# A fused attention and expert kernel: GpSimd takes the division of the probabilities in batch 0's attention, VectorE half of the copies to xT, and the global block's transposes another PSUM pool

## Chip, cores and metric

One core of a Trainium2 chip runs the whole program. The metric is the device time of one execution in microseconds, the median of three runs. The engines are PE (TensorE, with PEld for its weight loads), DVE (VectorE), ACT (ScalarE), POOL (GpSimd) and SP, whose queue issues the DMAs.

## What is computed

The reference is attention with a local window and a few global keys, followed by a mixture of eight experts whose gate is balanced by eight rounds of row and column scaling, followed by one dense feed-forward layer. Everything is float32. There are 2 batches of 768 positions, 8 heads of width 64, 8 global keys and a window of 96.

```python
def _attn_ref(q, k, v, n_global, n_local):
    scores = scale * np.matmul(q, k.transpose(0, 1, 3, 2))
    ...
    scores = np.where(keep, scores + bias, -1e9)      # keep: global key, or 0 <= i - j < n_local
    a = np.exp(scores - np.max(scores, axis=-1, keepdims=True))
    a = a / (np.sum(a, axis=-1, keepdims=True) + 1e-09)
    return np.matmul(a, v).astype(np.float32)

x = attn_out.transpose(0, 2, 1, 3).reshape(1536, 512)
# _moe_ref
for e in range(8):
    out += P[:, e:e + 1] * (np.maximum(x @ w1[e], 0.0) @ w2[e])     # w1[e] 512x1024
# _moe2_ref
h = out @ w_in                                                      # 512x2048
return (h * (1.0 / (1.0 + np.exp(-1.702 * h))) @ w_out).astype(np.float32)
```

## The kernel before

**Numbers.** Every product is made of three float32r products: an operand is split into a high part `h` and a rest `l`, and `l*h + h*l + h*h` is accumulated in PSUM. `split` (L207) makes the pair: the high part on the engine named by `eng`, the rest, a subtraction, on GpSimd or VectorE.

**Attention in tiles.** A tile is 128 queries of two heads, `(b, hp, i)`: batch, pair of heads (0 to 3), and one of six tiles. `work` lists them in this order, so batch 0 is the first 24. Below, tile 15 is `work[15]`, which is (0, 2, 3) and appears in names as `2_3`. A tile sees its own 128 keys, the 128 before, and 32 that hold the global ones: 288 columns, 256 for i=1 and 128 for i=0. Its steps are these:

- `scores`: six matmuls, then for each of the two heads VectorE adds the bias and finds the row's maximum (L1014) and ScalarE takes the exponential and the row's sum `rs` (L1017).
- `norm`: VectorE adds 1e-9 to `rs` (L1024), takes the reciprocal (L1025) and multiplies the two heads' probabilities by it (two instructions of L1027).
- `turn`: PE transposes the probabilities into the bank `pt` (L1038) and, from i=2 on, the global block into `pg` (L1046). ScalarE copies them out (`ah`, `ag`). The function that it returns makes the rest `al` on VectorE (L1059).
- `values`: PE multiplies by v into `pv` (L1079). After every odd i, `put_x` copies the two heads of two tiles to xT, here called `xf`, by two instructions on ScalarE (L851).

**The loop.** Step n of the loop at L1097 handles four tiles at once: the scores of tile n, the division of tile n-1, the transposes of tile n-3 and the product with v of tile n-4. The string `ORDER[self.phase]` says in which order (`t` turn, `s` scores, `v` values, `r` the rest, `n` norm). The order of instructions on each engine is the order in which the program writes them. After steps with i=1 and i=4 `prep_qk` transposes the next half pair's keys and queries (`pk`, `pq`), after i=2 and i=5 `prep_v` splits v on GpSimd (L214, L216).

**What is woven in.** `scores`, `values` and others are generators, and at their yields the loop in `path` (L1230) moves two others on: `first`, which prepares the first expert weights on GpSimd (sums, splits, and at the end the splits `w2h`/`w2l`), and `early`, which prepares the expert's operands from `xf` (`B11`, `T1`, later `B21`, `B22`, `T2` to `T4`, several of them through L298 and L216 on GpSimd). `self.phase` is 1 while tiles 0 to 21 leave through `values`, thus through batch 0's attention. Then the mixture starts (phase 2 and 3), in which batch 1's attention is woven into the expert products of batch 0, and later only expert and dense products are left.

**Banks.** PSUM has four pools of banks: `ps_s` 2, `ps_t` 2, `ps_v` 1, `ps_m` 3. `psum` (L638) chooses by a letter. In phase 1 the scores take `ps_m`, `pk` and `pq` take `ps_s`, and `pt` and `pg` take turns in `ps_t`.

Of the kernel before, what the change touches and what calls it, by code (L numbers as in the profile page):

```python
# [11 lines left out]
AF = mybir.ActivationFunctionType  # L12
ALU = mybir.AluOpType
# [3 lines left out]
P = 128  # L17
GK = 32
# [6 lines left out]
LR = 2  # L25


ORDER = {1: "tsvrn", 2: "stnrv", 3: "stnrv"}


def f(t):
    return t.bitcast(F32)
# [16 lines left out]
class Kernel:  # L49
# [588 lines left out]
    def psum(self, kind, shape, name):  # L638

        if kind == "r":  # L640
            kind = "m" if self.idle else "t"
        if kind == "2":
            self.turnover += 1
            kinds = {2: "m", 3: "sst", 4: "sstt"}[self.phase]
            kind = kinds[self.turnover % len(kinds)]
        elif self.phase == 1:
            kind = {"s": "m", "p": "s"}.get(kind, kind)
        kind = "t" if kind == "p" else kind
        p = {"s": self.ps_s, "t": self.ps_t, "v": self.ps_v, "m": self.ps_m}[kind]
        return p.tile(shape, F32, tag=kind, name=name)  # L650

# [190 lines left out]
    def put_x(self, pv, b, hp, i):  # L842


        nc = self.nc
        if hp == 0 and i == 1:
            self.xf = self.xfp.tile([P, self.DC, self.S], F32, tag="xf", name=f"xf_{b}")
        ts_ = slice((i - 1) * P, (i + 1) * P)
        for j in range(2):
            r = slice(64 * j, 64 * j + 64)  # L850
            nc.scalar.activation(self.xf[r, hp, ts_].rearrange("p (s t) -> p s t", s=2), pv[r, :, j, :], AF.Copy)  # L851

    def slope(self, h):
        return 2.0 ** -(8.0 * (h + 1) / self.H)
# [166 lines left out]
    def norm(self, b, hp, i):  # L1021
        nc = self.nc
        a, rs, wn = self.aa[b, hp, i]
        nc.vector.tensor_scalar(rs, rs, 1e-9, None, op0=ALU.add)  # L1024
        nc.vector.reciprocal(rs, rs)  # L1025
        for j in range(2):
            nc.vector.tensor_scalar(a[:, j, :wn], a[:, j, :wn], rs[:, j : j + 1], None, op0=ALU.mult)  # L1027

    def turn(self, b, hp, i):

        nc = self.nc
        a, _, _ = self.aa.pop((b, hp, i))
        n = 1 if i == 0 else 2
        pt = self.psum("t", [P, n, 2, P], f"pt_{b}_{hp}_{i}")
        for j in range(2):
            for c in range(n):
                o = c * (P if i == 1 else SLOT)
                nc.tensor.transpose(pt[:, c, j, :], a[:, j, o : o + P], self.ident)  # L1038
        ah = self.a_t.tile([P, 2, 2, P], F32R, tag="ah", name=f"ah_{b}_{hp}_{i}")
        al = self.a_t.tile([P, 2, 2, P], F32R, tag="al", name=f"al_{b}_{hp}_{i}")  # L1040
        nc.scalar.activation(ah[:, :n], pt, AF.Copy)
        ag = None
        if i >= 2:
            pg = self.psum("t", [GK, 2, P], f"pg_{b}_{hp}_{i}")
            for j in range(2):
                nc.tensor.transpose(pg[:, j, :], a[:, j, P:SLOT], self.ident)  # L1046

            if b == 0:
                ag = self.a_t.tile([GK, 2, P], F32, tag="ag", name=f"ag_{b}_{hp}_{i}")
                nc.scalar.activation(ag, pg, AF.Copy)  # L1050
            else:

                ag = self.a_t.tile([3 * GK, 2, P], F32R, tag="ag", name=f"ag_{b}_{hp}_{i}")
                nc.scalar.activation(ag[:GK], pg, AF.Copy)
                nc.scalar.activation(ag[2 * GK :], pg, AF.Copy)
        self.at[b, hp, i] = ah, al, ag

        def rest():
            nc.vector.tensor_tensor(out=al[:, :n], in0=pt, in1=f(ah)[:, :n], op=ALU.subtract)  # L1059
            if ag is not None and b > 0:  # L1060
                nc.vector.tensor_tensor(out=ag[GK : 2 * GK], in0=pg, in1=f(ag)[:GK], op=ALU.subtract)

        return rest
# [19 lines left out]
    def attention_banded(self):  # L1083

        nc = self.nc
        self.aq, self.av, self.vg = {}, {}, {}
        self.aa, self.at = {}, {}
        pairs = [(b, hp) for b in range(self.B) for hp in range(self.HP)]
        work = [(b, hp, i) for b, hp in pairs for i in range(self.NT)]
        tables = self.tables()  # L1090
        next(tables)
        self.scales()
        self.counts()
        next(tables)
        yield from self.prep_qk(0)
        next(tables)
        for n in range(len(work) + LV):  # L1097
            b, hp, i = work[n] if n < len(work) else (None, None, None)
            pair = n // self.NT
            rest = None  # L1100
            for o in ORDER[self.phase]:
                if o == "s" and i is not None:
                    yield from self.scores(b, hp, i)
                    if n == 0:
                        self.prep_v(0)
                if o == "t" and LT <= n < len(work) + LT:
                    rest = self.turn(*work[n - LT])
                if o == "n" and 1 <= n <= len(work):
                    self.norm(*work[n - 1])
                if o == "r" and rest is not None:  # L1110
                    rest()
                    yield
                if o == "v" and n >= LV:
                    self.values(*work[n - LV])
                    yield work[n - LV]
            if i == 1:
                yield from self.prep_qk(2 * pair + 1)
            if i == 4 and pair + 1 < len(pairs):
                yield from self.prep_qk(2 * pair + 2)
            if i == 2:  # L1120
                self.prep_v(2 * pair + 1)
            if i == 5 and pair + 1 < len(pairs):
                self.prep_v(2 * pair + 2)
# [246 lines left out]
```

## Time and profile before

| | |
|---|---|
| median of 3 runs | 1449.24 us (1448.56 to 1450.29) |
| profiled execution, its own time | 1451.42 us |
| its span, first to last instruction | 1449.5 us |
| busy share of the span: PE, DVE, POOL, ACT | 97%, 69%, 59%, 44% |
| mean granted TensorE clock | 0.993 |
| chain that ended last, by engine | PE 83%, DVE 10%, ACT 4%, issue 2%, POOL 1% |

The profiled execution is one more run, and what lies around its span is 1.92 us. Busy shares are means over all stages: batch 0's attention fills only about the first 95 us. The granted clock is 1.0 at 2.4 GHz and 0.5 at 1.2 GHz.

### The profile page before, as it was taken

How to read it: one execution, taken by the hardware profiler on the slowest of the kernel's cores; microseconds unless marked ns; L12 is line 12 of the kernel's file. 1: busy time of each engine (PE TensorE's matmuls, PEld its weight loads, DVE VectorE, ACT ScalarE, POOL GpSimd, SP SyncE). 2: the span in 40 equal slices, each digit the busy share in tenths (PEclk: the TensorE clock that was granted, in tenths of full speed). 3: DMA queues.
4: the chain of work that ended last, by engine and by line, in shares of the span. 5: the costliest groups of instructions: out<-in, count | busy, mean ns of one | idle time of the engine just before them, and what ended most of it. 6: DMA issues, size and time to landing. Idle time of an engine off the chain costs nothing.

```text
span 1449.5 us, 20861 instructions
## 1 busy us (share of the span) xinstructions
PE 1403.4 (97%) x7295; PEld 1239.3 (86%) x7295; DVE 1003.4 (69%) x1880; ACT 638.6 (44%) x1528; POOL 855.0 (59%) x999
## 2 busy tenths in 40 slices
PE   6899999899999999999999999999999988999998
PEld 5568888788898998998998998998989977898997
DVE  7987886667767777777677777777655464556655
ACT  5676766343443343333343333343333365444332
POOL 4755555756875666554666555666554567566642
PEclk9999999999999999999999999999999999999999
DMA  6322210111131222221222221222100100010002
GB/s 154 76 59 62 72 49 31 59 59 59 64 118 58 71 84 88 73 74 51 85 76 87 73 70 55 83 77 87 45 30 29 45 29 16 30 44 30 30 1 88
DMA packets 92626, 89.53 MB, mean 62 GB/s; under 512 B 41824, under 2 KB 70496, under 8 KB 92512
## 3 DMA queue, kind: packets, MB, share of 16 engines
q1 hardware_dynamic: 92512, 88.12, 19.5%
q8 instruction: 59, 0.97, 0.3%
q14 instruction: 55, 0.45, 0.1%
HBM read 76.56 MB, written 11.53 MB: 61 GB/s over the span
## 4 chain that ended last, share of the span: by engine, by line
PE 83%; DVE 10%; ACT 4%; issue 2%; POOL 1%; POOLq 0%; DVEq 0%; ACTq 0%
PE pl L558 41%; PE pl1y L503 11%; PE pl1x L503 11%; PE pl1z L503 10%; PE pl1w L503 5%; PE pv L1079 2%; PE s L1001 1%; DVE hl L482 1%; DVE a L1027 1%; DVE u L455 1%; DVE a L1014 1%; DVE al L1059 1%; PE pt L1038 1%; ACT hh L479 1%; PE plg L373 0%
## 5 line engine op out<-in xcount | busy, mean ns | idle before, releaser
L569 DVE SCALAR_TENSOR_TENSOR acc<-pl,pr,acc 128x512 f32<-128x512 f32 x312 | 233.4, 749 | 117.4 <-PE pl L558 115.2
L558 PE MATMUL pl<-w2h,hl 128*128 128x512 f32 x960 | 301.6, 395 | 5.9 <-DVE accx L567 2.4
L558 PE MATMUL pl<-w2h,hh 128*128 128x512 f32 x960 | 297.6, 391 | 3.3 <-ACT hh L210 2.8
L558 PE MATMUL pl<-w2l,hh 128*128 128x512 f32 x960 | 297.5, 391 | 0.0
L216 POOL TENSOR_TENSOR w2l<-r,w2h 128x512 fp32r<-128x512 f32 x96 | 128.7, 1362 | 194.4 <-ACT w2h L210 181.3
L558 PEld LDWEIGHTS pl<-w2h,hh 128*128 128x128 f32 x960 | 180.3, 188 | 42.7 <-ACT hh L210 3.1
L558 PEld LDWEIGHTS pl<-w2l,hh 128*128 128x128 f32 x960 | 180.5, 188 | 39.4
L558 PEld LDWEIGHTS pl<-w2h,hl 128*128 128x128 f32 x960 | 176.4, 188 | 40.1 <-DVE accx L567 3.8
L210 ACT ACTIVATE w2h<-r 128x512 fp32r<-128x512 f32 x94 | 54.3, 625 | 193.9 <-PE pl L558 163.0
L477 POOL TENSOR_TENSOR hl<-u,hh 128x384 fp32r<-128x384 f32 x100 | 106.9, 1078 | 38.4 <-ACT hh L474 38.2
L510 ACT ACTIVATE p<-pl1x 128x384 f32<-128x384 f32 x80 | 39.2, 490 | 162.3 <-PE pl1x L503 143.8
L477 POOL TENSOR_TENSOR hl<-p,hh 128x384 fp32r<-128x384 f32 x50 | 50.9, 1018 | 100.6 <-ACT hh L474 100.6
L216 POOL TENSOR_TENSOR hl<-sg,hh 128x384 fp32r<-128x384 f32 x64 | 65.3, 1021 | 59.4 <-ACT hh L210 58.4
L455 DVE TENSOR_TENSOR u<-p,pl1y 128x384 f32<-128x384 f32 x86 | 47.5, 552 | 70.4 <-PE pl1y L503 62.5
L473 ACT ACTIVATE p<-p 128x384 f32<-128x384 f32 x50 | 26.3, 527 | 137.3 <-DVE p L455 137.3
L482 DVE SCALAR_TENSOR_TENSOR hl<-pl1x,hh 128x384 fp32r<-128x384 f32 x64 | 35.6, 556 | 68.8 <-ACT hh L479 68.5
L216 POOL TENSOR_TENSOR S3l<-s,S3h 128x256 fp32r<-128x256 f32 x48 | 36.6, 764 | 69.9 <-ACT S3h L210 61.6
L203 POOL TENSOR_TENSOR s<-r 128x256 f32<-128x256 f32 x96 | 77.3, 806 | 0.0
L473 ACT ACTIVATE u<-u 128x384 f32<-128x384 f32 x100 | 51.9, 519 | 51.0 <-DVE u L455 50.8
L1017 ACT ACTIVATE a<-a,m 128x288 f32<-128x288 f32 (+2 forms) x96 | 48.1, 502 | 42.5 <-DVE m L1014 42.5
L575 DVE TENSOR_TENSOR acc<-pl,acc 128x512 f32<-128x512 f32 x84 | 54.2, 682 | 13.7 <-PE pl L558 12.7
L455 DVE TENSOR_TENSOR u<-u,pl1w 128x384 f32<-128x384 f32 x74 | 40.9, 552 | 21.9 <-PE pl1w L503 21.2
(283 smaller groups left out, 3411.1 us busy)
## 6 DMA issues: line engine op xcount, KB each, us to landing
r<-in_moe_w_dram SPq DMA_DIRECT2D x80, 512.0 KB, 3.5
d<-in_moe_w_in_dram SPq DMA_DIRECT2D x16, 512.0 KB, 4.6
d<-cx SPq DMA_DIRECT2D x32, 256.0 KB, 2.3
d<-in_moe_w_out_dram SPq DMA_DIRECT2D x16, 512.0 KB, 4.3
r<-d SPq DMA_DIRECT2D x16, 512.0 KB, 3.7
out_dram<-acc SPq DMA_DIRECT2D x12, 256.0 KB, 2.0
k<-in_k_dram SPq DMA_DIRECT2D x28, 96.0 KB, 2.6
q<-in_q_dram SPq DMA_DIRECT2D x28, 96.0 KB, 2.5
```

The costliest lines, as they stand in the source:

```text
L203: nc.gpsimd.tensor_tensor(out=o, in0=x, in1=y, op=op)
L210: nc.scalar.activation(hi, x, AF.Copy)
L216: e.tensor_tensor(out=lo, in0=x, in1=f(hi), op=ALU.subtract)
L455: add = lambda o, x, y: nc.vector.tensor_tensor(out=o, in0=x, in1=y, op=ALU.add)
L473: nc.scalar.activation(c, c, AF.Relu)
L477: nc.gpsimd.tensor_tensor(out=l, in0=c, in1=f(h), op=ALU.subtract)
L482: nc.vector.scalar_tensor_tensor(out=l, in0=c, scalar=0.0, in1=f(h), op0=ALU.max, op1=ALU.subtract)
L503: nc.tensor.matmul(ps, x[:, d, :], y[:, d, :], start=(new and i == 0 and d == 0), stop=(i == 2 and d == 1), skip_group_check=True)
L558: nc.tensor.matmul(ps, x[:, c, ts_], y, start=(n == 0 and c == 0), stop=(n == 2 and c == 1))
L569: nc.vector.scalar_tensor_tensor(out=acc, in0=ps, scalar=self.pr[:, tt, e : e + 1], in1=acc, op0=ALU.mult, op1=ALU.add)
L575: nc.vector.tensor_tensor(out=acc, in0=ps, in1=acc, op=ALU.add)
L1017: nc.scalar.activation(s, s, AF.Exp, bias=m, scale=-1.0, accum_out=rs[:, j : j + 1])
```

## The change

Three edits hold in phase 1, which is batch 0's attention. First, `norm`'s two multiplications move from VectorE to GpSimd, and the addition of 1e-9 becomes a step of its own, `epsilon`, also on GpSimd, that stands at the head of each step (`e`). The reciprocal stays on VectorE. Second, in `put_x` the second head's copy goes to VectorE. Third, `pg` gets the letter `g`, which in phase 1 is `ps_s`, where `pk` and `pq` are. In phases 2 and 3 the addition only changes its place in the code, just ahead of the reciprocal as before.

```diff
-ORDER = {1: "tsvrn", 2: "stnrv", 3: "stnrv"}
+ORDER = {1: "etsvrn", 2: "stenrv", 3: "stenrv"}
...
         elif self.phase == 1:
-            kind = {"s": "m", "p": "s"}.get(kind, kind)
-        kind = "t" if kind == "p" else kind
+            kind = {"s": "m", "p": "s", "g": "s"}.get(kind, kind)
+        kind = "t" if kind in "pg" else kind
...
-            nc.scalar.activation(self.xf[r, hp, ts_].rearrange("p (s t) -> p s t", s=2), pv[r, :, j, :], AF.Copy)
+            o = self.xf[r, hp, ts_].rearrange("p (s t) -> p s t", s=2)
+            if self.phase == 1 and j:
+                nc.vector.tensor_copy(o, pv[r, :, j, :])
+            else:
+                nc.scalar.activation(o, pv[r, :, j, :], AF.Copy)
...
         a, rs, wn = self.aa[b, hp, i]
-        nc.vector.tensor_scalar(rs, rs, 1e-9, None, op0=ALU.add)
         nc.vector.reciprocal(rs, rs)
         for j in range(2):
-            nc.vector.tensor_scalar(a[:, j, :wn], a[:, j, :wn], rs[:, j : j + 1], None, op0=ALU.mult)
+            x = a[:, j, :wn]
+            if self.phase == 1:
+                nc.gpsimd.tensor_scalar(x, x, rs[:, j : j + 1], 1.0, op0=ALU.mult, op1=ALU.mult)
+            else:
+                nc.vector.tensor_scalar(x, x, rs[:, j : j + 1], None, op0=ALU.mult)
+
+    def epsilon(self, b, hp, i):
+        rs = self.aa[b, hp, i][1]
+        if self.phase == 1:
+            self.nc.gpsimd.tensor_scalar(rs, rs, 1e-9, None, op0=ALU.add)
+        else:
+            self.nc.vector.tensor_scalar(rs, rs, 1e-9, None, op0=ALU.add)
...
-            pg = self.psum("t", [GK, 2, P], f"pg_{b}_{hp}_{i}")
+            pg = self.psum("g", [GK, 2, P], f"pg_{b}_{hp}_{i}")
...
+                if o == "e" and 1 <= n <= len(work):
+                    self.epsilon(*work[n - 1])
```

On GpSimd, around step 16, the rows of before are work of `first` and `early` alone. L952 copies global keys, `wg` is the gate's weights, and `acc_101` holds T1.

```order
L214 TENSOR_SCALAR S4h_20297<-s_0_19839 128x256
L216 TENSOR_TENSOR S4l_20298<-s_0_19839,S4h_20297 128x256
L214 TENSOR_SCALAR B11h_20282<-xf_19748 128x768
L216 TENSOR_TENSOR B11l_20283<-xf_19748,B11h_20282 128x768
L166 TENSOR_SCALAR wg_94<-wg 128x4x8
L167 TENSOR_TENSOR wg_94<-wg,wg_94 128x4x8
L214 TENSOR_SCALAR w2h_0_20341<-r_0_19564 128x512
L216 TENSOR_TENSOR w2l_0_20342<-r_0_19564,w2h_0_20341 128x512
L214 TENSOR_SCALAR T1h_20290<-acc_101 128x768
L216 TENSOR_TENSOR T1l_20291<-acc_101,T1h_20290 128x768
L952 TENSOR_SCALAR kh<-kh 128x3x32
```

The same place after the change, where L1039 is `epsilon` and L1032 are the two multiplications:

```order
L1032 TENSOR_SCALAR a_2_2_20212<-a_2_2_20212,rs_2_2_20213 128x288 x2
L1039 TENSOR_SCALAR rs_2_3_20259<-rs_2_3_20259 128x2
L214 TENSOR_SCALAR B11h_20283<-xf_19749 128x768
L216 TENSOR_TENSOR B11l_20284<-xf_19749,B11h_20283 128x768
L166 TENSOR_SCALAR wg_94<-wg 128x4x8
L167 TENSOR_TENSOR wg_94<-wg,wg_94 128x4x8
L214 TENSOR_SCALAR w2h_0_20342<-r_0_19565 128x512
L216 TENSOR_TENSOR w2l_0_20343<-r_0_19565,w2h_0_20342 128x512
L214 TENSOR_SCALAR T1h_20291<-acc_101 128x768
L216 TENSOR_TENSOR T1l_20292<-acc_101,T1h_20291 128x768
L1032 TENSOR_SCALAR a_2_3_20258<-a_2_3_20258,rs_2_3_20259 128x288 x2
```

The work of `first` and `early` now stands between the addition for tile 15 (`2_3`) and its multiplications, and the addition for the next tile comes behind both.

On VectorE the rows of before, at the end of step 15 and in step 16, are:

```order
L1059 TENSOR_TENSOR al_2_0_20255<-pt_2_0_20251,ah_2_0_20254 128x256
L1024 TENSOR_SCALAR rs_2_2_20212<-rs_2_2_20212 128x2
L1025 RECIPROCAL rs_2_2_20212<-rs_2_2_20212 128x2
L1027 TENSOR_SCALAR a_2_2_20211<-a_2_2_20211,rs_2_2_20212 128x288 x2
L1014 ISA a_2_4_20313,m_2_4_0_20319<-s_2_4_0_20315,bias 128x288
```

After the change the same place has these rows; L1018, L1073 and L1028 are the old L1014, L1059 and L1025, and L853 is the copy to xT:

```order
L853 COPY xf_19749<-pv_1_4_20228 64x256
L1073 TENSOR_TENSOR al_2_0_20256<-pt_2_0_20252,ah_2_0_20255 128x256
L1028 RECIPROCAL rs_2_2_20213<-rs_2_2_20213 128x2
L1018 ISA a_2_4_20314,m_2_4_0_20320<-s_2_4_0_20316,bias 128x288
L298 TENSOR_TENSOR acc_101<-xf_19749 128x768
```

Three instructions of each step are gone from VectorE, one copy has come in every second step, and the reciprocal, which stays, now needs a result of GpSimd.

## Rows read from the trace of the kernel before

**Rows 1.** The page's part 1: engine, busy time (share of the span), instructions.

```profile
PE 1403.4 (97%) x7295; PEld 1239.3 (86%) x7295; DVE 1003.4 (69%) x1880; ACT 638.6 (44%) x1528; POOL 855.0 (59%) x999
```

**Rows 2.** The chain that ended last, from 24 to 97 us: shares by line.

```profile
by line: DVE a L1027 15.9%; PE pv L1079 13.2%; DVE a L1014 11.7%; DVE al L1059 9.7%; issue 6.3%; PE s L1001 6.1%; ACT a L1017 4.7%; DVE kl L939 4.3%; ACT xf L851 3.7%; DVE rs L1024 3.7%; DVE ql L949 3.6%; PE pt L1038 3.3%; DVE rs L1025 2.4%
```

**Rows 3.** Line L1027: durations in ns, least/median/most.

```profile
L1027 DVE TENSOR_SCALAR a<-a,rs x96: 273/370/1969, 15.2 to 230.6; 128x288 f32<-128x288 f32 x64, 128x128 f32<-128x128 f32 x16, 128x256 f32<-128x256 f32 x16
```

**Rows 4.** VectorE in order of time: start us, us. Reciprocals of tiles 0, 12, 17, 21, 23.

```profile
14.98 0.17 DVE L1025 RECIPROCAL rs<-rs 128x2 f32<-128x2 f32 x1
...
50.35 0.17 DVE L1025 RECIPROCAL rs<-rs 128x2 f32<-128x2 f32 x1
...
70.60 0.17 DVE L1025 RECIPROCAL rs<-rs 128x2 f32<-128x2 f32 x1
...
84.10 0.17 DVE L1025 RECIPROCAL rs<-rs 128x2 f32<-128x2 f32 x1
...
91.15 0.17 DVE L1025 RECIPROCAL rs<-rs 128x2 f32<-128x2 f32 x1
91.35 1.48 DVE L1027 TENSOR_SCALAR a<-a,rs 128x288 f32<-128x288 f32 x2
```

**Rows 5.** The chain in order of time: start us, us; two score products three steps apart.

```profile
30.33 0.56 PE s L1001 x6
...
39.08 0.60 PE s L1001 x6
```

**Rows 6.** GpSimd in order of time: start us, us, work, idle before it.

```profile
48.55 0.32 POOL L952 TENSOR_SCALAR kh<-kh 128x96 fp32r<-128x96 f32 x1
...
54.21 0.84 POOL L214 TENSOR_SCALAR B11h<-xf 128x768 fp32r<-128x768 f32 x1
...
61.20 0.83 POOL L214 TENSOR_SCALAR T1h<-acc 128x768 fp32r<-128x768 f32 x1 [1.78 <-DVE acc L298]
...
64.95 0.27 POOL L952 TENSOR_SCALAR kl<-kl 128x96 fp32r<-128x96 f32 x1 [0.71 <-DVE kl L939]
...
69.02 0.72 POOL L203 TENSOR_TENSOR s<-r 128x256 f32<-128x256 f32 x1
...
71.72 0.79 POOL L203 TENSOR_TENSOR s<-r,s 128x256 f32<-128x256 f32 x1
...
84.79 1.04 POOL L216 TENSOR_TENSOR B22l<-xf,B22h 128x384 fp32r<-128x384 f32 x1 [1.05 <-ACT B22h L210]
...
89.12 1.00 POOL L216 TENSOR_TENSOR T2l<-acc,T2h 128x384 fp32r<-128x384 f32 x1 [0.89 <-ACT T2h L210]
...
93.43 0.29 POOL L973 TENSOR_SCALAR vg<-vl 32x128 fp32r<-32x128 f32 x1
```

**Rows 7.** Groups of GpSimd's instructions, 24 to 95 us: busy us, mean ns.

```profile
L216 POOL TENSOR_TENSOR vl<-v,vh 128x384 fp32r<-128x384 f32 x7 | 7.0, 1006 | 0.6
L214 POOL TENSOR_SCALAR vh<-v 128x384 fp32r<-128x384 f32 x7 | 3.6, 515 | 4.5 <-PE pv L1079 4.5
...
L214 POOL TENSOR_SCALAR w2h<-r 128x512 fp32r<-128x512 f32 x2 | 1.2, 620 | 0.0
...
L214 POOL TENSOR_SCALAR A11h<-r 128x256 fp32r<-128x256 f32 x1 | 0.4, 404 | 0.0
```

**Rows 8.** Line L434, a GpSimd multiplication by a scalar per row: ns, least/median/most.

```profile
L434 POOL TENSOR_SCALAR acc<-acc,pr x6: 700/855/1132, 359.4 to 369.8; 128x512 f32<-128x512 f32 x6
```

**Rows 9.** Stretch, length, busy us of PE, PEld, DVE, ACT, POOL, PEclk, DMA, GB/s.

```profile
54.00:66.00 12.00, 7.62 (x55) 5.31 (x53) 11.79 (x28) 5.79 (x19) 9.10 (x13) 1.00 0.37 94
66.00:75.00 9.00, 8.20 (x36) 5.78 (x36) 7.80 (x24) 5.27 (x18) 7.36 (x12) 0.62 0.29 82
105.00:115.00 10.00, 8.85 (x28) 7.45 (x29) 8.42 (x20) 4.46 (x12) 3.27 (x4) 0.51 0.01 2
```

**Rows 10.** PE's weight loads, 24 to 95 us: waits, us in total, times, longest.

```profile
PEld pg L1046 <- DVE al L1059: 5.4, 5, 2.1
```

**Rows 11.** Line L1061, VectorE reading PSUM in batch 1's attention: ns.

```profile
L1061 DVE TENSOR_TENSOR ag<-pg,ag x16: 412/414/416, 122.3 to 236.2; 32x256 fp32r<-32x256 f32 x16
```

## Prediction

> **What bounds the kernel now.** I read the page's busy shares first. PE is busy for 97% of the span [rows 1], so over the whole a microsecond counts only where PE waits. The change works in batch 0's attention alone, so the second view is the chain of waits from 24 to 97 us. It is mixed there: VectorE's multiplications (L1027) have 15.9% of the 73 us and its additions (L1024) 3.7%, together 14.3 us [rows 2]. Third, the line of the multiplications: the same instruction takes 273 ns or 1969, with a median of 370 [rows 3]. Fourth, GpSimd in order of time, for what runs on it then, and fifth the reciprocals as clock of the stage: one per tile. From tile 0's to tile 23's they stand at 14.98, 50.35 (tile 12), 70.60 (17), 84.10 (21) and 91.15 us [rows 4]. So tiles 1 to 12 took 35.37 us, tiles 13 to 17 took 20.25, tiles 18 to 21 took 13.50, and tiles 22 and 23 took 7.05. Where the chain is PE alone, three steps take 39.08 - 30.33 = 8.75 us, 2.92 a step [rows 5]. That is the pace to which a freed VectorE could bring the stage.
>
> **What the change does to the order.** On GpSimd each interval between two reciprocals now holds: the multiplications of tile k-1, the work of `prep`, the addition for tile k, the work of `first` and `early`, and then the multiplications of tile k. GpSimd can't start the last before VectorE's reciprocal of k, and VectorE can't pass that reciprocal before GpSimd's addition for k. Behind it on VectorE stand the next tile's maxima, for which ScalarE's exponentials wait, and the rests `al`, for which PE's product with v waits. So no interval can be shorter than GpSimd's work in it. Before, nothing tied GpSimd: it ran ahead of its place in the program. `B11h` of step 16 started at 54.21, so early that `T1h` behind it had to wait 1.78 us for VectorE to reach that step [rows 6]. That lead goes.
>
> **Prices.** GpSimd's one-input instruction takes 404 ns for 256 columns and 620 for 512 [rows 7], so 0.84 ns a column: 431 ns for 288, 296 for 128, and about 190 for the 2 columns of the addition. For a tile's pair I take 0.90 us with its pick-up (0.60 for i=0), for the addition 0.20. No row has this instruction with a scalar per row at this width. The nearest, 512 columns, has a median of 855 ns [rows 8], which scaled by 431/620 gives 594 ns: the upper bound, 1.19 us a pair. The lower bound is the 256-column row, 404.
>
> **The sum, stretch by stretch.**
>
> Tiles 1 to 12: GpSimd has little work here, and most intervals go at PE's pace: 12 x 2.92 = 35.0, a gain of 0.4. The intervals with v's split come close to that pace (0.52 + 1.01 [rows 7] + 0.90 + 0.20 = 2.63 and two hand-overs). I keep 2 us to either side, four intervals by half a microsecond, as an estimate.
>
> Tiles 13 to 17: GpSimd's work from 48.55 to 69.02 is 20.47 us less two waits of 1.78 and 0.71 [rows 6], 18.0. Added are four pairs at 0.90, one at 0.60 and five additions at 0.20: 23.2 against 20.25, a loss of 2.95. With the upper price it is 4.35; with the additions for nothing, 1.95.
>
> Tiles 18 to 21: GpSimd has 3.49 us from 69.02 to the end of the row at 71.72 [rows 6], then v's split (1.52) and a split like `vl` (1.01) [rows 7], 3.3 of multiplications and 0.8 of additions, 10.1 in all. PE needs 4 x 2.92 = 11.7, of which one step can be done ahead while VectorE waits for GpSimd, so 8.8. But its clock was 0.62 in the mean from 66 to 75 us [rows 9]: 6.8 us at 1.2 GHz, of which half, 3.4, is lost. With that 12.2. I take 11.5, between the two and nearer to the second: a gain of 2.0. Bounds: 10.1 (a gain of 3.4), and 11.7 + 3.4 = 15.1 (a loss of 1.6).
>
> Tiles 22 and 23: from 84.79 to 93.72 GpSimd has 8.93 us less a wait of 0.89 [rows 6], 8.04. With two pairs, two additions, and 0.25 less for the head start of the first split: 10.0 against 7.05, a loss of 2.95. Bounds 2.0 (the first split wholly ahead) and 3.6 (the upper price).
>
> After tile 23: on VectorE the two multiplications of 1.48 us [rows 4] no longer stand between its reciprocal and the maxima of tile 25, for which ScalarE's queue then waited. A gain of 1.5 (bounds 0 and 1.5). GpSimd has until the next reciprocal about 1.0 + 0.9 + 0.2, which is hidden behind those maxima and the rest `al`.
>
> **The other two edits cost nothing.** The copies: no row has a copy from PSUM on VectorE. The nearest, 32x256 out of PSUM, takes 414 ns and varies by 4 [rows 11]. There are 11, so 4.5 us, on an engine that is rid of 14.3; were VectorE still last, up to 4.5 would come back. The banks: PE's waits of `pg` for the rest, 5.4 us in 5 [rows 10], go, since `pt` has both banks of its pool. But they were waits for a late VectorE, which GpSimd's pace now replaces. If the cover is gone, `pg` waits for ScalarE's copy of the one before, which is long done.
>
> The sum is -0.4 + 2.95 - 2.0 + 2.95 - 1.5 = +2.0 us. Behind this stage PE is the bound, so the shift stays to the end. The profiled execution, 1449.5 of span and 1451.42 in all, would become 1453.4. The median of the runs shown is 2.2 lower, and the forecast is made on it: **1451.2 us**. About 0.2%, 2.9 us, is what a measurement of this kernel tells from no change, so I call this no change.
>
> **Rivals.**
>
> *Slower, by TensorE's clock (1456.6).* Place: the interval of tile 16, where `B11`, `w2h` and `T1` stand between addition and multiplications, and those of 22 and 23. In tile 16's, GpSimd has 64.95 - 0.71 - 54.21 - 1.78 = 8.25 us [rows 6] and 1.1 of division, over three times PE's step, so PE idles; in 22 and 23 PE has 5.8 us of work in 10, 58%. Before the fall to 1.2 GHz now, PE was busy for 7.62 of 12 us, 64% [rows 9]. If each stall is followed by a spell as long as the present one, tiles 18 to 21 keep their 13.5 (+2.0) and the start of the mixture loses 3.4. It decides from the point where the spell lies outside the stall itself.
>
> *Slower, by the price (1455.6).* If GpSimd takes twice VectorE's undisturbed 370 ns [rows 3], 0.74, a pair costs 1.48, 0.58 more. That adds 2.6 in tiles 13 to 17, 1.2 in 22 and 23, and 0.6 in 18 to 21, where GpSimd's 12.1 passes my 11.5. Against it: the one-input rows give 431. By a rule this is what to expect: the Trainium skill, GPSIMD Engine Reference, in its opening, calls GpSimd the wrong choice for ordinary elementwise arithmetic, with VectorE about twice as fast. By that rule the kernel ends slower; this trace agrees with it only in part, 404 ns for 256 columns against 370 for mostly 288.
>
> *Faster, by the clock (1444.9).* If PE is busy enough that no spell falls into tiles 18 to 21, GpSimd's 10.1 sets them (-1.4), and if the mixture's spell from 105 to 115 us (0.51 in the mean over 10 us, 4.9 lost [rows 9]) doesn't come either. For it: VectorE no longer holds PE in the light intervals. Against it: the stall of tile 16.
>
> *Much faster (1438.7).* GpSimd keeps its lead and all goes at PE's pace: 14.6, 11.7 and 5.8 for the three later stretches, so -0.4 - 5.65 - 1.8 - 1.2 - 1.5. Against it stands the order of GpSimd's queue.
>
> That VectorE is relieved and merely waits instead is no rival but the forecast itself.
>
> **Chances.** The forecast 0.40, slower by the clock 0.22, by the price 0.10, by the upper bounds together 0.06, faster by the clock 0.15, much faster 0.07. So faster 0.22, same 0.40, slower 0.38. The range from 1444 to 1457.5 takes in the two clock cases and the price, and leaves out the much faster case and the upper bounds together.
>
> **What would show it.** Right: VectorE's reciprocals wait for GpSimd's additions, above all at tile 16 (some 4 to 6 us) and at 22 and 23; GpSimd is busy nearly without a gap from tile 13 to 17; tile 12's reciprocal comes within 2 us of 50.35, tile 17's some 2 to 3 us later than 70.60, tile 23's at about 94.7. L1032 takes 0.43 us for 288 columns. Wrong: if tile 16's interval is under 6 us, GpSimd's work doesn't bind it; if L1032 is over 0.6, the price was wrong; if `pv` still takes twice its usual time at tile 23 and after, it is the clock.

## The result and the profile after

The changed kernel takes **1468.76 us** (median of 4 runs, 1464.48 to 1469.12), the kernel before beside it 1449.39. The ratio is 1.0117, 95% interval 1.0105 to 1.0129: slower by about 17 us (the two medians lie 19.4 apart), outside the range that was given. The profiled execution is the fastest of the four, 1464.48 with a span of 1462.7; the 4 us by which the others are longer are in no trace, and the rows account for 13.2 of the 17.

Part 1 of the page after, to be read against [rows 1]: VectorE lost 24 us of work, GpSimd took up 25, and PE did the same work in a span that is 13 us longer.

```profile
PE 1405.9 (96%) x7295; PEld 1239.5 (85%) x7295; DVE 979.2 (67%) x1818; ACT 635.1 (43%) x1517; POOL 880.2 (60%) x1072
```

VectorE in order of time after, the reciprocals of tiles 0, 12, 16, 17, 21 and 23 (start us, us; in brackets the idle time before it and what ended it), to be read against [rows 4]:

```profile
13.79 0.16 DVE L1028 RECIPROCAL rs<-rs 128x2 f32<-128x2 f32 x1
...
53.73 0.15 DVE L1028 RECIPROCAL rs<-rs 128x2 f32<-128x2 f32 x1
...
74.28 0.17 DVE L1028 RECIPROCAL rs<-rs 128x2 f32<-128x2 f32 x1 [4.21 <-POOL rs L1039]
79.43 0.17 DVE L1028 RECIPROCAL rs<-rs 128x2 f32<-128x2 f32 x1 [2.80 <-POOL rs L1039]
...
93.23 0.17 DVE L1028 RECIPROCAL rs<-rs 128x2 f32<-128x2 f32 x1 [0.47 <-POOL rs L1039]
...
104.12 0.17 DVE L1028 RECIPROCAL rs<-rs 128x2 f32<-128x2 f32 x1 [4.41 <-POOL rs L1039]
```

Tile 23's comes 12.97 us later than before, so practically the whole loss of this execution arises in batch 0's attention, and PE, which bounds the rest, carries it to the end. Differences of these rows against those of [rows 4] give the table that the rest of the text uses (us):

| stretch | before | predicted | after |
|---|---|---|---|
| tiles 1 to 12 | 35.37 | 35.0 | 39.94 |
| tiles 13 to 17 | 20.25 | 23.2 | 25.70 |
| tiles 18 to 21 | 13.50 | 11.5 | 13.80 |
| tiles 22 and 23 | 7.05 | 10.0 | 10.89 |

Waits of the kernel after from 20 to 110 us (engine, line, waited for: us in total, times, longest):

```profile
DVE rs L1028 <- POOL rs L1039: 18.9, 10, 4.4
...
DVE xf L853 <- ACT xf L855: 13.7, 11, 1.8
...
PEld pt L1052 <- POOL a L1032: 10.1, 11, 4.9
...
PEld pg L1060 <- DVE kl L943: 8.2, 7, 1.4
```

Three edits, and each has left a wait. VectorE waits for GpSimd's addition, and PE's transposes wait for GpSimd's multiplications (the division). VectorE's half of the copy waits for ScalarE's half, at every one of the 11 copies. The transposes of the global block wait for `kl`, in place of `al` as in [rows 10]. Which of them costs the time no list of waits can say; that is what the experiments are for.

Stretches of the kernel after (stretch, length, busy us of PE, PEld, DVE, ACT, POOL, then the granted clock), to be read against [rows 9]:

```profile
42.00:54.00 12.00, 9.21 (x67) 6.53 (x65) 6.44 (x24) 8.43 (x27) 9.86 (x22) 1.00 0.26 59
54.00:66.00 12.00, 9.07 (x59) 5.95 (x61) 7.75 (x24) 6.76 (x21) 11.08 (x22) 0.95 0.42 105
66.00:75.00 9.00, 4.42 (x22) 3.19 (x24) 2.13 (x7) 2.37 (x8) 8.54 (x13) 0.50 0.10 21
75.00:82.00 7.00, 7.00 (x32) 5.21 (x30) 2.06 (x10) 2.72 (x10) 6.57 (x12) 0.50 0.22 54
...
105.00:115.00 10.00, 7.82 (x55) 6.37 (x54) 7.52 (x25) 6.58 (x21) 6.08 (x11) 1.00 0.28 62
115.00:130.00 15.00, 11.90 (x57) 9.66 (x57) 11.86 (x27) 8.41 (x22) 4.85 (x7) 0.77 0.07 15
```

GpSimd is busy nearly without a gap from 54 to 75 us while VectorE is idle for half of it (7.75 and 2.13 us busy in 21), and the clock is at its lower level from 66 to 82 us; with the 0.95 of the stretch before, it fell at about 64.9, so it was down for 17 us, where it was for 6.8 before. An earlier spell, 3.4 us near 25, is not in these lines. The stretch from 105 to 115, at 0.51 before, is at full clock, but its spell has not gone. It comes later, as the whole kernel does, and lasts some 6.9 us (0.77 over the last 15) where before it was 9.8 (0.51 over 10).

PE's longest wait comes from tile 15's division. On GpSimd in order of time (tile 14's multiplications, the first and the last of a block of eight instructions, tile 15's multiplications, and further on tile 17's addition and multiplications), and on PE the transposes of tiles 15 and 17:

```profile
63.27 0.99 POOL L1032 TENSOR_SCALAR a<-a,rs 128x288 f32<-128x288 f32 x2
...
64.64 0.83 POOL L214 TENSOR_SCALAR B11h<-xf 128x768 fp32r<-128x768 f32 x1
...
70.70 1.80 POOL L216 TENSOR_TENSOR T1l<-acc,T1h 128x768 fp32r<-128x768 f32 x1
72.49 0.99 POOL L1032 TENSOR_SCALAR a<-a,rs 128x288 f32<-128x288 f32 x2
...
79.18 0.21 POOL L1039 TENSOR_SCALAR rs<-rs 128x2 f32<-128x2 f32 x1
...
80.19 0.98 POOL L1032 TENSOR_SCALAR a<-a,rs 128x288 f32<-128x288 f32 x2
```

```profile
73.05 1.17 PE L1052 MATMUL pt<-ident,a 128*128 128x128 f32 x4 [4.58 <-POOL a L1032]
...
83.41 0.60 PE L1052 MATMUL pt<-ident,a 128*128 128x128 f32 x4
```

From 64.64 to 72.49, 7.85 us, GpSimd works through `B11`, `wg`, `w2` and `T1`, and the multiplications stand behind them. The reciprocal itself was there at 64.59. PE's wait of 4.58 us runs from 68.47 to 73.05, so the clock, which fell at 64.9, fell ahead of it and not behind it. GpSimd goes on after the block: from tile 12's multiplications at 54.44 to the end of tile 17's addition at 79.39 it is never idle for over 0.1 us, so these intervals are its work and nothing else. The reciprocals of tiles 16 and 17 wait for it.

The price of the division by form, the first two lines GpSimd after from 24 to 110 us, the third the same product on VectorE before, from 24 to 95 (busy us, mean ns | idle before):

```profile
L1032 POOL TENSOR_SCALAR a<-a,rs 128x288 f32<-128x288 f32 x28 | 13.9, 505 | 5.5 <-DMA q<-in_q_dram 3.6 <-DVE rs L1028 1.9
L1039 POOL TENSOR_SCALAR rs<-rs 128x2 f32<-128x2 f32 x20 | 4.3, 213 | 1.7
```

```profile
L1027 DVE TENSOR_SCALAR a<-a,rs 128x288 f32<-128x288 f32 x28 | 15.9, 610 | 0.5
```

And the copy, VectorE and ScalarE after, in order of time:

```profile
31.92 0.36 ACT L855 ACTIVATE xf<-pv 64x256 f32<-64x256 f32 x1
...
32.31 0.43 DVE L853 COPY xf<-pv 64x256 f32<-64x256 f32 x1 [1.14 <-ACT xf L855]
...
32.77 0.69 DVE L1073 TENSOR_TENSOR al<-pt,ah 128x512 fp32r<-128x512 f32 x1
```

The two halves write different partitions of one `xf`, yet VectorE's starts only when ScalarE's has ended. Both also read one bank, `pv`; whether the common `xf` or the common `pv` makes the wait, no run tells. ScalarE has it behind its exponentials, so VectorE idles 1.14 us, and `al`, the maxima and the next reciprocal stand behind it.

### The profile page after: what moved, and what is told of

The parts are those of the page before. It is cut to its first block, busy times and chain, and to the rows that moved or that the text cites. A ratio compares the mean times of both kernels' runs of the same rounds, so it can differ in the third digit from the quotient of the medians.

```text
span 1462.7 us, 20927 instructions
## 1 busy us (share of the span) xinstructions
PE 1405.9 (96%) x7295; PEld 1239.5 (85%) x7295; DVE 979.2 (67%) x1818; ACT 635.1 (43%) x1517; POOL 880.2 (60%) x1072
## 3 DMA queue, kind: packets, MB, share of 16 engines
q1 hardware_dynamic: 92512, 88.12, 18.9%
## 4 chain that ended last, share of the span: by engine, by line
PE 82%; DVE 7%; ACT 3%; POOL 3%; issue 2%; SPq 1%; DMA 0%; ACTq 0%; DVEq 0%; POOLq 0%
PE pl L558 41%; PE pl1y L503 11%; PE pl1x L503 11%; PE pl1z L503 10%; PE pl1w L503 5%; PE pv L1093 2%; DVE hl L482 1%; DVE u L455 1%; PE s L1005 1%; SPq L929 1%; PE pt L1052 1%; ACT a L1021 1%; POOL a L1032 1%; ACT hh L479 1%; DVE sg L470 1%
## 5 line engine op out<-in xcount | busy, mean ns | idle before, releaser
L455 DVE TENSOR_TENSOR p<-u,pl1z 128x384 f32<-128x384 f32 x74 | 40.8, 551 | 21.7 <-PE pl1z L503 20.2
```

The costliest lines, as they stand in the source:

```text
L455: add = lambda o, x, y: nc.vector.tensor_tensor(out=o, in0=x, in1=y, op=ALU.add)
```

## The experiments

All times are medians, each ratio against the kernel before on the same chip, with its 95% interval. In the names, before is B and the changed kernel A.

### Each edit alone

Theory at this point: the division costs by the lock (VectorE can't pass a reciprocal before GpSimd's addition, GpSimd can't pass it the other way), and one of the other edits adds to it. The three runs are B with one edit each (left out below: the `else` branch of the copy, the letter's entry in `psum`):

```
e1:  -  nc.vector.tensor_scalar(rs, rs, 1e-9, ...)      +  epsilon() on gpsimd, ORDER "etsvrn"
     -  nc.vector.tensor_scalar(a[:, j, :wn], ...)      +  nc.gpsimd.tensor_scalar(x, x, rs[:, j : j + 1], 1.0, ...)
e2:  +  if self.phase == 1 and j: nc.vector.tensor_copy(o, pv[r, :, j, :])
e3:  -  pg = self.psum("t", ...)                        +  pg = self.psum("g", ...)
```

> The division alone goes to GpSimd; copies and banks are as before. Theory L (the lock: VectorE's reciprocal waits for GpSimd's addition): this edit carries most of the loss, 1457 to 1464 us, with VectorE's reciprocals waiting some 15 to 20 us for the additions. Theory C (the copies: VectorE's half waits for ScalarE's half, 11 times 1.2 us): the division costs little, 1448 to 1453, since the loss needs the copies. Theory B (the banks: pg waits for kl): the same, 1448 to 1453.

Measured: 1463.73 us, 1.0088 (1.0072 to 1.0105), as theory L had it. The reciprocals wait 30.3 us for the additions, more than the 15 to 20 expected.

> The copies alone are halved between ScalarE and VectorE. Theory C: slower by 8 to 17 us (1457 to 1466), since VectorE is last in this stage and each of 11 copies puts a wait of about 1.2 and 0.43 us of work on it. Theories L and B: 1449 to 1454.

Measured: 1474.49 us, 1.0171 (1.0152 to 1.0190): alone, the edit that was forecast at nothing costs 25 us, more than the whole change and more than the 17 that theory C allowed. Its clock was at the lower level for 48 us (summed over half microseconds from 12 to 145 us), against 17 before. Its waits, 20 to 110 us:

```profile
DVE xf L853 <- ACT xf L855: 13.6, 10, 2.4
PEld pg L1050 <- DVE al L1063: 11.5, 5, 3.5
```

> The bank of pg alone changes. Theory B: slower by 3 to 8 us (1452 to 1457), with pg waiting for kl about 7 times 1.2 us. Theories L and C: 1446 to 1450, the 5.4 us of waits for al go and nothing takes their place.

Measured: 1453.71 us, 1.0014 (1.0003 to 1.0025), 2 us and less than theory B's 3. `pg` no longer waits for `al` but now for the keys' rest, 10.7 us where [rows 10] had 5.4 (that row from 24 to 95 us, this one from 20 to 110):

```profile
PEld pg L1046 <- DVE kl L939: 10.7, 7, 3.4
```

### What the copies cost

e10 is e2 with the two halves exchanged, so that ScalarE waits for VectorE and not the other way; amounts of work are the same.

```
-  if self.phase == 1 and j:          +  if self.phase == 1 and not j:
```

> The copies alone, with the first half on VectorE and the second on ScalarE, so that VectorE's copy waits for PE alone and ScalarE's for VectorE. Theory C (VectorE's wait for ScalarE is the cost of the copies edit): most of the 25 us goes, leaving about 11 times 0.43 us, a ratio of 1.000 to 1.005. Rival V (VectorE can't carry the copies, or ScalarE's wait costs as much): 1.010 to 1.017.

Measured: 1457.45 us, 1.0046 (1.0030 to 1.0062). Three quarters of the 25 us hang on which half comes first: on the wait, and on what came with it, the lower clock too (21 us by the same sum, against 48). What remains, 6.7 us (4.4 to 9.0), is near to 11 copies by 428 ns, 4.7 us, on the engine that ends last in this stage. Its order of time:

```profile
31.53 0.42 DVE L853 COPY xf<-pv 64x256 f32<-64x256 f32 x1 [0.77 <-PE pv L1083]
31.98 0.38 ACT L855 ACTIVATE xf<-pv 64x256 f32<-64x256 f32 x1 [0.44 <-DVE xf L853]
```

e4 is A without the copies, e17 is A with the halves exchanged. Both ask what the copies cost inside the whole change.

```
e4:   -  (the copies' hunk)
e17:  -  if self.phase == 1 and j:    +  if self.phase == 1 and not j:
```

> The changed kernel without its copies edit: both copies are ScalarE's as before. Theory L: nearly as slow as the whole change, 1462 to 1468. Theory C: 1449 to 1455, most of the loss is gone. Theory B: about 1455 to 1460.

Measured: 1463.93 us, 1.0085 (1.0065 to 1.0105).

> The whole change with VectorE copying the first half and ScalarE the second. If VectorE's wait for ScalarE is what the copies cost inside the whole change: that of the division with the banks, 1.007 to 1.010. If the waits for GpSimd cover it there: unchanged, 1.0105 to 1.013.

Measured: 1463.53 us, 1.0092 (1.0075 to 1.0110). So inside the whole change the copies cost 1.0117 less 1.0085, 4.6 us, of which 1.0117 less 1.0092, 3.6 us, is the wait; by the intervals each of these differences is uncertain by some 3 us. Alone they cost five times as much. That fits a VectorE which after the division is seldom the engine that ends last.

### What the division costs

Theory L, the lock, against theory W: the multiplications stand in GpSimd's queue behind `B11` to `T1`, PE's transposes wait for them, and the lower clock follows. e8 is e1 with the addition on VectorE again, ahead of the reciprocal, e7 is A with the same edit. The addition's lock is gone, GpSimd's queue stays.

```
-  self.nc.gpsimd.tensor_scalar(rs, rs, 1e-9, ...)      +  self.nc.vector.tensor_scalar(rs, rs, 1e-9, ...)
-  1: "etsvrn"                                          +  1: "tsvren"
```

> The division alone, with the addition of 1e-9 back on VectorE just ahead of the reciprocal, so that VectorE waits for nothing of GpSimd and only the 48 multiplications are moved. Theory L (the lock through the addition makes the loss of the division): close to the kernel before, within 4 us, a ratio of 0.996 to 1.003. Rival W (GpSimd's sheer work in its queue, whose late multiplications hold up PE's transposes): still slower by 8 to 13 us, 1.0055 to 1.009.

Measured: 1462.80 us, 1.0068 (1.0051 to 1.0085).

> The whole change, with the addition of 1e-9 back on VectorE just ahead of the reciprocal. Theory L: what is left is the copies' part, 1.002 to 1.006. Rival W: as the whole change, 1.009 to 1.013.

Measured: 1467.55 us, 1.0102 (1.0085 to 1.0118). In both the gain, 2 to 3 us, is within the intervals. The longest entry in the list of waits has gone and hardly any time with it: VectorE now waits one instruction further on, for PE's scores, 24.0 us where e1 had 10.2. In e8, its wait, then GpSimd and PE in order of time:

```profile
DVE a L1014 <- PE s L1001: 24.0, 16, 7.8
```

```profile
59.82 0.83 POOL L214 TENSOR_SCALAR B11h<-xf 128x768 fp32r<-128x768 f32 x1
...
67.69 0.99 POOL L1028 TENSOR_SCALAR a<-a,rs 128x288 f32<-128x288 f32 x2
```

```profile
68.25 1.18 PE L1048 MATMUL pt<-ident,a 128*128 128x128 f32 x4 [6.19 <-POOL a L1028]
```

The block is the same 7.87 us without the lock. To tell W from the mere amount of work moved, three more runs put only some tiles' division on GpSimd (all with the addition on VectorE, no other edit):

```
-  if self.phase == 1:
+  if self.phase == 1 and 6 * hp + i < 14:                                    (e11)
+  if self.phase == 1 and 6 * hp + i >= 14:                                   (e12)
+  if self.phase == 1 and 6 * hp + i not in (14, 15, 16, 17, 22, 23):         (e13)
```

> Only the division of tiles 0 to 13 goes to GpSimd; the epsilon stays on VectorE ahead of the reciprocal, the copies and the banks stay as before. Theory W (the division alone loses its 10 us because tile 15's multiplications stand in GpSimd's queue behind the 7.9 us of B11, wg, w2 and T1, the transposes wait for them and TensorE then runs at 1.2 GHz): nothing of that kind stands ahead of tiles 0 to 13, so within 3 us of before: ratio 0.998 to 1.002, tile 12's reciprocal at 49.8 us, tile 17's within 1 us of 70.6. Rival A (every division on GpSimd costs its share, whatever stands in the queue): 14 of 24 of the 10 us, ratio 1.004.

Measured: 1450.85 us, 0.9996 (0.9986 to 1.0007). The ratio is W's; the places were not. Tile 12's reciprocal comes at 48.49 instead of 49.8, and that tile 17 would come within 1 us of 70.60 was wrong. Its reciprocal comes 2.59 us earlier, and by tile 23 only 0.33 us of it are left (91.15 before):

```profile
68.01 0.17 DVE L1024 RECIPROCAL rs<-rs 128x2 f32<-128x2 f32 x1
...
90.82 0.17 DVE L1024 RECIPROCAL rs<-rs 128x2 f32<-128x2 f32 x1
```

```profile
66.00:75.00 9.00, 9.00 (x35) 6.55 (x35) 6.93 (x21) 4.24 (x14) 8.40 (x13) 0.50 0.29 82
```

From 66 to 75 us its PE is busy throughout at the lower clock, 0.50 where before had 0.62 [rows 9]. The gain is given back there.

> The complement: only the division of tiles 14 to 23 goes to GpSimd. Theory W: nearly all of the loss, ratio 1.005 to 1.008, PE's transposes again wait over 5 us for GpSimd's multiplications near 62 to 68 us, and the granted clock falls to 0.50 behind it. Rival A: 10 of 24 of the 10 us, ratio 1.003.

Measured: 1458.44 us, 1.0046 (1.0030 to 1.0062), just under W's bound. The wait stands where W puts it:

```profile
66.12 1.18 PE L1048 MATMUL pt<-ident,a 128*128 128x128 f32 x4 [5.31 <-POOL a L1028]
```

But in this run the time is not lost there. Tile 17's reciprocal comes at 70.00 (70.60 before) and tile 23's at 91.78 (91.15). The loss stands behind that, at the other heavy tiles: at 92.26 PE has waited 1.48 us for tile 22's multiplications, from about 91.7 to 102 the clock is at its lower level, and the tile after next comes at 104.41 (98.97 before).

> The division goes to GpSimd except in tiles 14 to 17, 22 and 23, where GpSimd has the large splits of phase 1's weave. Theory W: the long waits of the transposes go, tiles 18 to 21 keep their gain of 1 to 2 us, ratio 0.996 to 1.001. Rival A: 18 of 24 of the 10 us, ratio 1.005.

Measured: 1451.83 us, 1.0002 (0.9992 to 1.0011). With 18 of 24 tiles' division on GpSimd nothing is lost, with the last ten tiles' 6.7 us are. Rival A, the amount, falls: by it e11 and e13 would be at 1.004 and 1.005. Tiles 18 to 21 did not keep a gain: from tile 17's reciprocal (68.09) to tile 21's (84.28) they took 16.19 where before had 13.50. Stretches of e13:

```profile
54.00:66.00 12.00, 8.60 (x53) 5.92 (x52) 11.79 (x27) 7.67 (x23) 11.50 (x15) 0.76 0.38 94
66.00:75.00 9.00, 9.00 (x36) 6.55 (x35) 5.53 (x19) 4.18 (x14) 7.62 (x14) 0.50 0.26 82
75.00:82.00 7.00, 7.00 (x42) 4.82 (x42) 4.71 (x16) 4.58 (x14) 2.58 (x5) 0.84 0.25 56
```

By its granted clock (0.76, 0.50, 0.84) the lower level lasted 17 us here, as long as in the changed kernel, without any long wait for GpSimd and without a loss. So of W the queue holds: the loss needs multiplications that stand behind large splits. Its last step, that the lower clock follows from that wait and makes the loss, is not borne out: here the clock fell without the wait. It isn't quite all: e11 and e12 together make 1.0042 and e8 1.0068, which their intervals just allow.

### Together

> Tiles 0 to 13's division on GpSimd (epsilon on VectorE) and the copies shared out with VectorE taking the first half and ScalarE the second, so that VectorE waits for nothing of ScalarE's. Theories W and C (the copies cost VectorE 0.43 us each where it ends last, and the wait for ScalarE that the swap takes away): VectorE gives up 0.99 us a tile in the first fourteen and takes up 0.43 every second tile, so it is the last engine only in tiles 14 to 23: ratio 0.999 to 1.004, below the 1.0046 of the swapped copies alone. Rival: the two add up whatever VectorE has free, ratio 1.005 to 1.008.

e14 is e11 with the copies exchanged as in e10. Measured: 1451.99 us, 1.0003 (0.9992 to 1.0013). The swapped copies, 1.0046 alone, cost nothing measurable where VectorE has been relieved.

The next three are A with parts undone:

```
e15:  the addition on VectorE, the tiles of e13, the copies exchanged
e16:  the addition on VectorE, the tiles of e13
e5:   -  pg = self.psum("g", ...)     +  pg = self.psum("t", ...)
```

> The whole change with both suspected waits taken out: tiles 14 to 17, 22 and 23 divide on VectorE as before, the epsilon is VectorE's, and VectorE copies the first half so that it does not wait for ScalarE. Theories W and C: what is left is the banks' 2 us and VectorE's copies where it still ends last, ratio 1.000 to 1.005. Rival (something else in the combination costs): 1.008 or more.

Measured: 1457.04 us, 1.0052 (1.0039 to 1.0066), at the edge of what was expected. VectorE divides the six heavy tiles again, is last there again, and the swapped copies and the banks cost about what they do alone (1.0046 and 1.0014). PE waits for the keys' rest:

```profile
PEld pg L1060 <- DVE kl L943: 10.8, 7, 4.7
```

> As the run before, but VectorE's copy is still the second half and waits for ScalarE's. Theory C: VectorE has its work of before in the six heavy tiles and loses up to 2.3 us at each copy there, and 1.6 us at the others where it has room; ratio 1.005 to 1.010. If VectorE's room after the division covers the wait, 1.000 to 1.004.

Measured: 1463.65 us, 1.0108 (1.0088 to 1.0128). That is a little above what was expected: the wait for ScalarE is worth 1.0108 less 1.0052, 8 us, in this setting. A longer spell of the lower clock has no part in that: by the same sum as for e2 it lasted 17 us in e16 and 21 in e15.

> The whole change without the shared banks. If the banks cost in the whole what they cost alone (2 us): ratio 1.0103; if VectorE's later keys make pg wait longer in the whole: 1.008 or less; if the wait is hidden behind the others: 1.0117 as the whole change.

Measured: 1474.18 us, 1.0174 (1.0160 to 1.0187), which none of the cases gave: inside the whole change the shared banks save 8 us.

> Copies and banks without the division. Theory G (the banks edit takes pg's wait for al away, which the copies make long): the copies' 1.0171 falls by about 6 us to 1.011 to 1.014, no wait of pg for al is left. Rival (the gain needs the division): 1.0171 plus 2 us, 1.018 to 1.019.

e6 is B with the copies and the banks. Measured: 1475.69 us, 1.0165 (1.0143 to 1.0187). So theory G, that the banks earn this by freeing `pg` of a late `al`, falls: with the copies alone they change nothing, although `pg` waits only for `kl` there (11.3 us), as the theory had it. What tells e5 from A most is the clock of two stretches in which tiles 9 to 15 lie, 0.76 and 0.67 against 1.00 and 0.95 above:

```profile
42.00:54.00 12.00, 10.08 (x59) 7.34 (x58) 5.52 (x21) 6.72 (x21) 10.59 (x25) 0.76 0.29 67
54.00:66.00 12.00, 12.00 (x60) 8.72 (x60) 5.58 (x20) 6.34 (x19) 7.45 (x17) 0.67 0.15 34
```

Tile 12's reciprocal is 4.84 us later in e5 (58.57 against 53.73). That alone does not make the 8 us: in e7, which has the shared banks, it comes at 58.17, and the ratio is 1.0102. Whether the waits bring the clock down or the clock lengthens the waits was not separated, and stays open.

No run beats the kernel before by more than its uncertainty; the lowest is e11.

## Why the prediction was wrong

**Failed: "The other two edits cost nothing."** The copies were priced by their duration (414 ns by the nearest row, 428 measured), and the work that was to hide them was named: a VectorE rid of 14.3 us. That held for the duration and missed a wait. VectorE writes the second half of a tile whose first half ScalarE writes, out of the same bank, and waits for ScalarE's copy, 11 times, 13.7 us. Alone this makes 1.0171, without the wait 1.0046; inside the whole change 4.6 us. It is also why tiles 1 to 12 took 39.94: in the six kernels with the wait (the changed one, e2, e5, e6, e7, e16) they took 39.9 to 45.9, in the eleven other runs 33.2 to 37.9. In e16 the clock was full in that stretch and they still took 40.97. The banks: "`pg` waits for ScalarE's copy of the one before, which is long done" was wrong. Those banks are the keys' and queries', which a step with `prep` fills first, and there `pg` waits for VectorE's `kl`. Alone that costs 2 us; inside the change it came with a saving of 8.

**Too small: the division.** Its sum was +2.0; without the copies it is 12 us (e4). The mechanism was the right one. GpSimd loses its lead, and its work sets the intervals: the block at tiles 15 and 16 holds VectorE's reciprocal (4.21 us; 4 to 6 were named) and PE's transposes. That interval was worked out at 8.25 and 1.1 of division and took 9.69 (64.59 to 74.28). Four terms were mis-sized:

- Tiles 13 to 17, "a loss of 2.95": 5.45, above the upper bound of 4.35. GpSimd worked without a gap, so the 2.5 us between are its own. Its splits and small copies took 18.7 us where the sum had 18.0 (`S4l` alone 0.78 more), the multiplications 4.5 for 4.2, the five additions with their hand-overs 1.8 for 1.0. And 0.7 of `S3`'s split, which ran ahead before and was left out of the sum, now stood behind tile 12's reciprocal (53.73 to 54.44).
- Tiles 18 to 21, "a gain of 2.0": a loss of 0.30. The term had PE one step ahead at tile 17 and the clock down for 6.8 us. The clock was down for 17, nearly all of it ahead of this stretch, and PE, at work without a gap from 73.05 to 84.0, was behind and not ahead.
- Tiles 22 and 23, "a loss of 2.95": 3.84, above the bound of 3.6. From 93.52 to 104.08 GpSimd is again never idle for over 0.1 us.
- After tile 23, "a gain of 1.5": the tile after next came 7.54 us after tile 23 (111.66 less 104.12), 7.82 before (98.97 less 91.15), a gain of 0.28.

"Slower, by TensorE's clock" gave 1456.6 and was right that the clock would be down for longer. Its condition, a spell behind each stall, was not met: the clock fell ahead of the stall of 4.58 us, and behind that of tiles 22 and 23 it was full. By the prediction's own sign, `pv` at tile 23 and after (0.28 us a product at full clock, 0.41 in the spell), it is not the clock.

**Right:** the places, tiles 13 to 17 and 22 to 23, GpSimd busy there without a gap, and the prices within their bounds. A product of 288 columns took 505 ns (431 taken, 594 the upper bound), an addition 213 (200). "Slower, by the price" is out: in the six heavy tiles 12 products by 74 ns make 0.9 us. The rule that stood behind that rival, the opening of the GPSIMD Engine Reference in the Trainium skill, is narrowed by the same page's section on engine selection, where the factor of two is for two inputs and one-input work is called roughly line-rate. The trace lies between the two and nearer to the latter: 505 against an undisturbed 370 [rows 3], 1.36 times, and below the 610 that VectorE really took here in the mean.

"Faster, by the clock" hoped for full clock in tiles 18 to 21 and in the start of the mixture. The mixture's spell came all the same, some 3 us shorter, and nothing came of that: behind tile 23 the shift grew from 12.97 to the span's 13.2.

**Not told apart:** how much the lower clock adds to the division's 12 us. In tiles 13 to 17 and 22 to 23, the main part, GpSimd's work alone fills the time. Between them the clock can have put off PE by 2.2 us at most, an estimate from two rows of the changed kernel: tile 17's multiplications end at 81.17 and its transposes begin at 83.41. In e12, where the addition is VectorE's, a wait of 1.48 us and a spell of lower clock come together behind tile 22, and no run parts them.

## What to carry to other kernels

Work that is moved to an engine that looks idle joins the end of its queue. What counts is the length of the block ahead of it at the step where another engine waits, not its price: 18 of 24 tiles were moved at no loss (e13), and with the other six it was 10 us (e8). Ask of every split across two engines whether the halves share a tile or a bank, and in which order they run. If one half must wait for the other, the engine that ends last takes the first half (1.0046 against 1.0171 for the copies alone). An entry at the head of the list of waits is no cause: 18.9 us of waits for the addition were taken away for a gain within the error.

## What the runs showed of the hardware

GpSimd and VectorE hold each other up. GpSimd's `S4l` took 0.73 us before and 1.51 after, where VectorE's addition L298 with two inputs ran beside it (the first line is before, the others after):

```profile
53.51 0.73 POOL L216 TENSOR_TENSOR S4l<-s,S4h 128x256 fp32r<-128x256 f32 x1
```

```profile
61.77 1.51 POOL L216 TENSOR_TENSOR S4l<-s,S4h 128x256 fp32r<-128x256 f32 x1
```

```profile
61.74 0.95 DVE L298 TENSOR_TENSOR acc<-xf 128x768 f32<-128x768 f32 x1
```

The excess, 0.78, is near to the length of L298. The Trainium skill, SBUF — State Buffer, on the two sides of SBUF, says that the two engines share a port pair as an exclusive lock, held for the whole instruction; these rows agree. VectorE's 1969 ns beside GpSimd's splits [rows 3] are gone with the product.

TensorE's clock stayed at its lower level for stretches of very different length: 6.8 us before, 17 in the changed kernel, where it fell ahead of the long stall, and 17 in e13, where PE's longest waits were under 2 us. It also stayed there while PE was busy throughout: 7.00 of 7 us in the changed kernel (75 to 82), 9.00 of 9 in e11 and e13 (66 to 75). And the spell of 17 us went with a loss in one kernel and, in sum, with none in the other, so its length is no price either.
